# Products of zeros in TensorE's waits through the whole prologue, from a held attention PSUM bank, and the last output tile copied and stored by two engines

## The chip, the cores and the metric

The kernel runs on one core of a Trainium2 chip. The metric is the device time of one launch in microseconds (us). A profiled execution also gives a span, from its first instruction to its last; the time of a launch is about 1.7 us longer than that.

## The reference

A linear-attention recurrence (RWKV-6 style) over 4 batches, 8 heads, 768 steps and head dimension 48, followed by a two-layer MLP on the 3072 rows of 384 that it gives:

```python
def _attn_ref(r, k, v, w, u):
    state = zeros((B, H, D, D)); y = zeros_like(r)
    for t in range(S):
        cur = einsum('bhd,bhe->bhde', u[None] * kt, vt)
        y[:, :, t] = einsum('bhd,bhde->bhe', rt, state + cur)
        state = wt[:, :, :, None] * state + einsum('bhd,bhe->bhde', kt, vt)
    return y

def _moe_ref(x, w_in, w_out):        # x: (3072, 384)
    h = x @ w_in                     # (3072, 2048)
    g = np.maximum(0.01 * h, h)
    return (g @ w_out)               # (3072, 384), float32
```

All inputs are float32; the kernel's matrix products take bfloat16.

## The kernel before, in words

**Attention.** The sequence is cut into 24 chunks of 128 steps (6 a batch). For chunk i the steps are: `log` of the decays w (ScalarE), `cum` (TensorE: running sums of the logs by a triangular matrix, into a PSUM bank), `exp` and `neg`/`exn` (e to the sum and to its negative), `kr` (VectorE: k and r scaled by them, bf16), `trans` (TensorE: eight transposes into the tile `trp`) and `rkT` (their copy to SBUF), `scores` (TensorE, two banks `at`), `m0` and `m1` (VectorE: causal mask), `mix` (TensorE: scores times v, plus the carried state, into `y`), `ysb` (VectorE: y plus the diagonal part), `kv`, `tt` and `st` (the state update: TensorE, VectorE or ScalarE, GpSimd), and `ytr` and `xT` (transposed y as the MLP's input, resident in SBUF). GpSimd computes `t1`, `t2` and `vsc`, VectorE `diag`, for the diagonal part. The first four chunks (EARLY) take another form of `log` and `cum`, from two loads `wp` of two chunks each, and get `neg` from TensorE through a bank of the MLP pool.

**MLP.** The rows are taken in 15 blocks q of 128 or 256. `hid` (q, j) is a group of hidden products for some of the 16 hidden tiles from j on, into a PSUM tile `hp`; `act` is the leaky ReLU out of it (ScalarE); `out` multiplies the result by w_out into a tile `op`. `m_copy` (L479) copies an output tile of 128 x 384 from PSUM to SBUF on ScalarE and `m_store` (L483) issues its store from ScalarE's DMA queue. The weights are loaded in four quarters each and cast to bf16 by VectorE (`cast`).

**PSUM.** Eight banks: the pool `ps_att` has five (tag "att"), `ps_mlp` three (tag "mlp").

**The order.** All instructions are listed with engine, planned duration, needs and the PSUM banks that they take until some later step ends. The class `Order` simulates this list: it repeatedly takes the step that can start first, and keeps for each pool a list of slots with the step that will free each. The kernel is then emitted in exactly that order, and every engine runs its instructions in it. Loads go out on SyncE's DMA queue (SP), as do the transposing DMAs that replace `trans` from chunk 10 and `ytr` from chunk 18 on.

**Zero products.** At emission, before each TensorE step whose predecessor on TensorE ends before WARM (18.0 us of the plan), the planned gap is filled with products of a tile of zeros, `idle`, into the PSUM tile `scratch`: one for each planned 0.45 us before 6.0 us, and for each 0.22 us after it, every one of 512 columns. `scratch` has one of the three MLP banks, a fact that the planner isn't told of.

Of the kernel before, what the change touches and what calls it, by code (L numbers as in the profile page):

```python
# [8 lines left out]
F32 = mybir.dt.float32  # L9
# [6 lines left out]
class Order:  # L16
# [7 lines left out]
    def add(self, name, eng, took, f, *args, lag=0.06, rank=0.0, needs=(), takes=()):  # L24
        self.steps[name] = (eng, took, f, args, lag, rank, list(needs), takes)
# [11 lines left out]
    def run(self, pools):  # L37
        ends, out = {}, []
        self.times = []
        free = {}  # L40
        slots = {p: [None] * n for p, n in pools.items()}
        place = {}
        todo = {}
        for seq, (name, s) in enumerate(self.steps.items()):
            todo.setdefault(s[0], []).append((s[5], seq, name))
        for eng in todo:
            if eng != "DMA":
                todo[eng].sort()
            free[eng] = 0.0
        free["DMA"] = 0.85  # L50

        def ready(name):
            t = 0.0
            for n in self.steps[name][6]:
                n = self.real(n)
                if n not in ends:
                    return None
                same = self.steps[n][0] == self.steps[name][0] != "DMA"
                t = max(t, ends[n] - (self.steps[n][4] if same else 0.0))
            for pool in slots:  # L60
                n = sum(p == pool for p, _ in self.steps[name][7])
                if n:
                    freed = [x for x in slots[pool] if x is None or x in ends]
                    if len(freed) < n:
                        return None
                    freed.sort(key=lambda x: -1 if x is None else place[x])
                    t = max([t] + [ends[x] for x in freed[:n] if x is not None])
            return t

        while any(todo.values()):  # L70
            best = None
            for eng, names in todo.items():
                loads = False
                for rank, seq, name in names:
                    waits = name[0] in ("store", "rkT", "xT")
                    if eng == "DMA" and not waits:
                        if loads:
                            continue
                        loads = True
                    t = ready(name)  # L80
                    if t is None:
                        continue
                    if eng == "DMA" and waits and loads:
                        t += self.slack[name[0]]
                    t = max(t, free[eng])
                    key = (t, rank, seq)
                    if best is None or key < best[0]:
                        best = (key, eng, (rank, seq, name))
            assert best is not None, {e: n[:3] for e, n in todo.items()}
            (t, _, _), eng, item = best  # L90
            todo[eng].remove(item)
            _, took, f, args, lag, _, _, takes = self.steps[item[2]]
            free[eng] = t + took
            ends[item[2]] = t + took + lag
            place[item[2]] = len(place)
            for pool, until in takes:
                freed = [x for x in slots[pool] if x is None or x in ends]
                oldest = min(freed, key=lambda x: -1 if x is None else place[x])
                slots[pool].remove(oldest)
                slots[pool].append(self.real((until, item[2][1]) if isinstance(until, str) else until))  # L100
            out.append((f, args))
            self.times.append((t, t + took, eng))
        self.ends, self.free = ends, free
        return out
# [3 lines left out]
def kernel(  # L108
# [11 lines left out]
    nc = tc.nc  # L120
    B, H, S, D = r.shape
# [9 lines left out]
    NOUT = moe_w_out.shape[1]  # L131
# [3 lines left out]
    NQ = 4  # L135
# [7 lines left out]
    opool = ctx.enter_context(tc.tile_pool(name="opool", bufs=NOUTB))  # L143
    ps_att = ctx.enter_context(tc.tile_pool(name="ps_att", bufs=5, space=bass.MemoryType.PSUM))
    ps_mlp = ctx.enter_context(tc.tile_pool(name="ps_mlp", bufs=3, space=bass.MemoryType.PSUM))
# [6 lines left out]
    idle = const.tile([128, 512], BF16, name="idle")  # L152
# [92 lines left out]
    att = {i: {} for i in range(NCH)}  # L245
# [202 lines left out]
    starts = [sum(sizes[:n]) for n in range(len(sizes))]  # L448
    gts = {}
    hps = {}  # L450
    ops = {}
    osbs = {}
# [23 lines left out]
                start=(j == 0), stop=(j == NFT - 1),  # L476
            )

    def m_copy(q, ts):  # L479
        osb = osbs[q, ts] = opool.tile([128, NOUT], F32, name="osb")  # L480
        nc.scalar.copy(out=osb[:], in_=ops.pop((q, ts))[:])  # L481

    def m_store(q, ts):  # L483
        row = starts[q] + ts * 128
        nc.scalar.dma_start(out=out[row : row + 128, :], in_=osbs.pop((q, ts))[:])

    def m_stored(q, ts):
        pass
# [2 lines left out]

    BY_DMA = range(10, NCH)
    Y_BY_DMA = range(18, NCH)
    WARM = 18.0
    OFF = {'exn': -1.5, 'log': -1.5, 'trans': -2.5, 'ytr': -0.5, 'exp': -2.5, 'scores': -0.5, 't2': 1.5, 't1': -2.5, 'ysb': 1.5, 'vb': 1.5, 'vsc': 1.5}
    RCAST = 5
    SLACK = 1.2
# [3 lines left out]
    add = order.add  # L501
# [6 lines left out]
    for kind, n in queue:  # L508
        past_user = users[-NIN:][:1] if len(users) >= NIN else []
        if kind == "in":  # L510
            if n < EARLY:
                order.alias(("w", n), ("wp", n // 2))
                if n % 2 == 0:
                    add(("wp", n // 2), "DMA", 1.35, load_wp, n // 2, lag=1.95,
                        needs=[("logp", n // 2 - 1)] if n else [])
# [65 lines left out]
    for q, mb in enumerate(sizes):  # L581
        nj = 512 // mb
        xs = [("xT", i) for i in range(starts[q] // L, (starts[q] + mb) // L)]
        for j in range(0, NFT, nj):
            add(("hid", q, j), "PE", nj * 3 * (mb / 2400 + 0.0035), m_hid, q, j, nj, lag=0.17, rank=100 + q,
                takes=(("mlp", ("act", q, j)),),
                needs=xs + [("cast", "w_in", (j + nj - 1) // JQ)] + ([("out", q - 2, sizes[q - 2] // L - 1, NQ - 1)] if q > 1 else []))
            add(("act", q, j), "ACT", nj * mb / 1200 + 0.17, m_act, q, j, nj, rank=RACT, needs=[("hid", q, j)])
        acts = [("act", q, j) for j in range(0, NFT, nj)]
        for ts in range(mb // L):  # L590
            for part in range(NQ):
                add(("out", q, ts, part), "PE", JQ * 0.163, m_out, q, ts, part, lag=0.17, rank=101.5 + q + 0.01 * ts,
                    takes=(("mlp", ("copy", q, ts)),) if part == 0 else (),
                    needs=[x for x in acts if x[2] < (part + 1) * JQ] + [("cast", "w_out", part)]
                    + ([("out", q, ts, part - 1)] if part else []))
            tiles.append((q, ts))
            add(("copy", q, ts), "ACT", 0.48, m_copy, q, ts, rank=0, needs=[("out", q, ts, NQ - 1)]
                + [("store", *x) for x in tiles[-NOUTB - 1 : -NOUTB]])
            add(("issue", q, ts), "ACT", 0.3, m_store, q, ts, rank=-1, needs=[("copy", q, ts)])
            add(("store", q, ts), "DMA", 0.6, m_stored, q, ts, lag=1.9, rank=-1, needs=[("issue", q, ts)])  # L600
    steps = order.run({"att": 5, "mlp": 3})
    with tc.manual_schedule():
        nc.scalar.preload_act_table_set("natural_log_exp_and_others")
        scratch = ps_mlp.tile([128, 512], F32, name="scratch", tag="mlp")
        at = 1.3
        for (f, args), (start, end, eng) in zip(steps, order.times):
            if eng == "PE" and at < WARM:
                for _ in range(int((start - at) / (0.45 if at < 6.0 else 0.22))):
                    nc.tensor.matmul(scratch[:], lhsT=idle[:, 0:128], rhs=idle[:], start=True, stop=True)  # L609
            if eng == "PE":  # L610
                at = end
            f(*args)
# [30 lines left out]
```

## Time and profile before

| | |
|---|---|
| median of 4 runs | 187.65 us |
| lowest, highest | 186.71, 189.6 us |
| the profiled execution: time | 186.71 us |
| the profiled execution: span | 185.0 us |
| TensorE busy | 176.7 us (96%) |
| zero products | 22 records, 8.2 us busy |
| hidden products (line 462) | 720, 72.1 us busy |
| output products (line 474) | 384, 69.5 us busy |

How to read it: PE is TensorE, PEld its weight loads, DVE is VectorE, ACT is ScalarE, POOL is GpSimd, SP is SyncE. In a list of instructions in order of time the first number is the start within the span and the second the length of the merged group, both in us; `x8` counts instructions; brackets give the idle time of the engine just before, and what ended it. [...] In the lists of waits the numbers are total us, times, and the longest.

### The profile page before, as it was taken

Reading aid. Unit: us, or ns where it says so; the run is one execution under the profiler, and the core shown is the slowest. Engines: PE = TensorE matmul, PEld = TensorE weight load, DVE = VectorE, ACT = ScalarE, POOL = GpSimd, SP = SyncE. Lnnn points to the kernel's source line nnn. Section 1 sums busy time; section 2 is a strip of 40 time slices with the busy share of each in tenths; the row PEclk is TensorE's granted clock in tenths of the full one; section 3 lists DMA queues with packets and bytes.
Section 4 is the critical chain, followed back from the end, with each engine's and each line's share of the span. In section 5 each row is a group of like instructions: output and inputs, shape, how many; then the busy total and the mean of one; then the engine's idle time right before and its main releaser. Section 6 shows DMA issues by size and latency. Waiting matters only on the chain.

```text
span 185.0 us, 4892 instructions
## 1 busy us (share of the span) xinstructions
PE 176.7 (96%) x1954; PEld 134.4 (73%) x1955; DVE 113.6 (61%) x187; ACT 113.2 (61%) x218; POOL 109.9 (59%) x144
## 2 busy tenths in 40 slices
PE   7999769999999999999999999999999999999992
PEld 1456558966879878688796688869785786887961
DVE  4368996494689987848495775657575573460000
ACT  3656858914857857677695478669573465662731
POOL 7568975406666799995748785865559268220000
PEclk9999999999999999999999999999999999999999
DMA  6999999999989999998979989899996999422102
GB/s 137 187 211 276 227 348 168 393 351 152 292 173 212 206 199 208 187 224 177 210 149 175 190 178 209 165 200 199 199 160 143 185 180 214 108 64 65 45 7 78
DMA packets 120696, 34.46 MB, mean 186 GB/s; under 512 B 115553, under 2 KB 118626, under 8 KB 120674
## 3 DMA queue, kind: packets, MB, share of 16 engines
q1 hardware_dynamic: 117216, 29.43, 81.8%
q10 hardware_dynamic: 3458, 4.72, 7.6%
q8 instruction: 15, 0.25, 0.6%
q14 instruction: 7, 0.06, 0.1%
HBM read 25.17 MB, written 4.72 MB: 162 GB/s over the span
## 4 chain that ended last, share of the span: by engine, by line
PE 81%; DMA 5%; POOL 4%; DVE 4%; issue 2%; ACT 2%; ACTq 0%; POOLq 0%; DVEq 0%
PE op L474 33%; PE hp L462 31%; PE at L367 3%; DMA rkT<-kr 3%; PE y L392 2%; DMA wp<-in_w_dram 2%; PE trp L346 2%; PE cum L282 2%; PE scratch L609 2%; POOL t L322 2%; PE y L386 2%; PE ytr L433 2%; PE kv L405 1%; DVE mt L375 1%; POOL t L318 1%
## 5 line engine op out<-in xcount | busy, mean ns | idle before, releaser
L462 PE MATMUL hp<-xT,w_in_b 128*128 128x256 bf16 (+1 forms) x720 | 72.1, 252 | 0.5 <-ACT xT L441 0.2
L468 ACT ACTIVATE gt<-hp 128x512 bf16<-128x512 f32 x96 | 56.9, 597 | 21.5 <-PE hp L462 18.2
L474 PE MATMUL op<-w_out_b,gt 128*128 128x384 bf16 x384 | 69.5, 326 | 0.0
L462 PEld LDWEIGHTS <-w_in_b 128*128 128x128 bf16 x720 | 62.8, 114 | 3.9 <-DVE w_in_b L239 0.9
L474 PEld LDWEIGHTS <-gt 128*128 128x128 bf16 x384 | 35.7, 98 | 20.0
L375 DVE TENSOR_TENSOR mt<-at,tri 128x512 bf16<-128x512 f32 x48 | 30.8, 683 | 10.4 <-PE at L367 10.2
L318 POOL TENSOR_TENSOR t<-in,ukb 128x384 f32<-128x384 f32 x24 | 24.0, 1002 | 17.6 <-DMA in<-in_r_dram 8.9
L314 DVE TENSOR_TENSOR kr<-e,in 128x768 bf16<-128x768 f32 x24 | 27.4, 1143 | 10.8 <-ACT e L310 9.6
L423 POOL TENSOR_TENSOR st<-tt,e 48x192 bf16<-48x192 f32 x40 | 22.6, 565 | 14.6 <-DVE tt L413 10.2
L337 POOL TENSOR_TENSOR vsc<-in,diag 128x384 f32<-128x384 f32 x24 | 23.4, 976 | 11.4 <-DVE diag L333 11.0
L322 POOL TENSOR_TENSOR t<-t,in 128x384 f32<-128x384 f32 x24 | 26.0, 1082 | 3.0 <-DMA in<-in_k_dram 1.7
L400 DVE TENSOR_TENSOR ysb<-y,vsc 128x384 bf16<-128x384 f32 x24 | 13.3, 552 | 11.6 <-PE y L392 7.8
L307 ACT ACTIVATE e<-cum 128x388 f32<-128x388 f32 x24 | 11.9, 494 | 13.6 <-PE cum L284 7.6
L481 ACT COPY osb<-op 128x384 f32<-128x384 f32 x24 | 11.4, 477 | 14.2 <-PE op L474 14.0
L329 POOL CAST vb<-in 128x384 bf16<-128x384 f32 x20 | 12.7, 635 | 7.1 <-DMA in<-in_v_dram 6.6
L300 DVE SCALAR_TENSOR_TENSOR neg<-cum,lw 128x384 f32<-128x384 f32 x20 | 11.0, 552 | 9.3 <-ACT e L307 9.1
L333 DVE TENSOR_REDUCE diag<-t 128x8 f32<-128x384 f32 x24 | 13.1, 544 | 5.0 <-POOL t L322 5.0
L254 ACT ACTIVATE lw<-in 128x384 bf16<-128x384 f32 x20 | 10.4, 520 | 5.6 <-DMA in<-in_w_dram 5.4
L310 ACT ACTIVATE e<-neg 128x384 f32<-128x384 f32 x20 | 10.5, 523 | 4.8 <-DVE neg L300 3.1
L441 ACT COPY xT<-ytr 128x384 bf16<-128x384 bf16 x18 | 8.6, 477 | 2.1 <-ACT osb L481 1.2
L367 PE MATMUL at<-rkT 48*128 48x128 bf16 x192 | 9.5, 219 | 0.2 <-DMA rkT<-kr 0.2
L609 PE MATMUL scratch<-idle 128*128 128x512 bf16 x22 | 8.2, 505 | 1.3 <-DVE idle L180 1.3
(55 smaller groups left out, 137.6 us busy)
## 6 DMA issues: line engine op xcount, KB each, us to landing
in<-in_r_dram SPq DMA_DIRECT2D x24, 192.0 KB, 4.4
in<-in_k_dram SPq DMA_DIRECT2D x24, 192.0 KB, 4.6
in<-in_v_dram SPq DMA_DIRECT2D x24, 192.0 KB, 4.7
out_dram<-osb ACTq DMA_DIRECT2D x24, 192.0 KB, 3.1
in<-in_w_dram SPq DMA_DIRECT2D x20, 192.0 KB, 4.7
ws<-in_moe_w_in_dram SPq DMA_DIRECT2D x4, 768.0 KB, 6.5
ws<-in_moe_w_out_dram SPq DMA_DIRECT2D x4, 768.0 KB, 6.5
wp<-in_w_dram SPq DMA_DIRECT2D x2, 384.0 KB, 4.4
```

The lines of the kernel that those rows point to most:

```text
L314: nc.vector.tensor_tensor(out=kr_b[i % NB3][:, :, 0:D], in0=e, in1=ins[i]["kr"], op=ALU.mult)
L318: nc.gpsimd.tensor_tensor(out=t1[:], in0=flat(ins[i]["r"]), in1=ukb[:], op=ALU.mult)
L322: nc.gpsimd.tensor_tensor(out=flat(t2[:]), in0=att[i]["t1"][:], in1=flat(ins[i]["k"]), op=ALU.mult)
L333: nc.vector.tensor_reduce(out=diag[:], in_=att[i]["t2"][:], axis=AX.X, op=ALU.add)
L337: nc.gpsimd.tensor_tensor(out=vsc[:], in0=ins[i]["v"], in1=att[i]["diag"][:].unsqueeze(2).to_broadcast([128, H, D]), op=ALU.mult,)
L367: nc.tensor.matmul(ats[x][:, p, :], lhsT=rkT[r0 : r0 + D, 0, p, :], rhs=rkT[r0 : r0 + D, 1, p, :], start=True, stop=True,)
L375: nc.vector.tensor_tensor(out=att[i]["mt"][:, x], in0=att[i]["ats"][x][:], in1=tri[:].unsqueeze(1).to_broadcast([128, NP, 128]), op=ALU.mult,)
L400: nc.vector.tensor_tensor(out=ysb[:], in0=att[i]["y"][:], in1=flat(att[i]["vsc"][:]), op=ALU.add)
L423: nc.gpsimd.tensor_tensor(out=sn[r0 : r0 + D, :, x * D : (x + 1) * D], in0=tt[r0 : r0 + D, :, x * D : (x + 1) * D], in1=el[r0 : r0 + D, :] ...
L462: nc.tensor.matmul(hp[:, jj, :], lhsT=w_in_b[:, wq, t, f0::JQ], rhs=xT[:, t, t0 : t0 + mb], start=(t == 0), stop=(t == KT - 1),)
L468: nc.scalar.activation(out=gts[q][:, j : j + nj, :], in_=hps.pop((q, j))[:], func=AF.Prelu, alpha=0.01)
L474: nc.tensor.matmul(ops[q, ts][:], lhsT=gts[q][:, j, ts * 128 : (ts + 1) * 128], rhs=w_out_b[:, j, :], start=(j == 0), stop=(j == NFT - 1),)
```

## The change

The zero products go on until 33.0 us of the plan. Each has 256 columns instead of 512, one for each planned 0.22 us where the gap begins before COLD (8.2 us), and for each 0.11 us after it. `scratch` moves to an attention bank, and the planner now knows: one of its five attention slots is held by a step `warm` that ends at 33 us. The two steps `cold` and `warm` on an engine of their own, `CLOCK`, do nothing but mark that time in the order.

The last output tile is split at column 192. ScalarE copies and stores the first half as before; a new VectorE step `copy2` copies the second half into a tile of its own, and `store2` issues its store from SyncE's queue.

```diff
@@ Order.run
         slots = {p: [None] * n for p, n in pools.items()}
+        slots["att"][0] = "warm"
@@ the output tile
-    def m_copy(q, ts):
+    HALF = NOUT // 2
+
+    def m_copy(q, ts, last):
         osb = osbs[q, ts] = opool.tile([128, NOUT], F32, name="osb")
-        nc.scalar.copy(out=osb[:], in_=ops.pop((q, ts))[:])
-
-    def m_store(q, ts):
+        n = HALF if last else NOUT
+        nc.scalar.copy(out=osb[:, 0:n], in_=ops[q, ts][:, 0:n])
+
+    def m_store(q, ts, last):
         row = starts[q] + ts * 128
-        nc.scalar.dma_start(out=out[row : row + 128, :], in_=osbs.pop((q, ts))[:])
+        n = HALF if last else NOUT
+        nc.scalar.dma_start(out=out[row : row + 128, 0:n], in_=osbs[q, ts][:, 0:n])
+
+
+    def m_copy2(q, ts):
+        osb = osbs["last"] = opool.tile([128, HALF], F32, name="osb2", bufs=1)
+        nc.vector.tensor_copy(out=osb[:], in_=ops[q, ts][:, HALF:])
+
+    def m_store2(q, ts):
+        row = starts[q] + ts * 128
+        nc.sync.dma_start(out=out[row : row + 128, HALF:], in_=osbs["last"][:])
@@ constants of the plan
-    WARM = 18.0
+    WARM = 33.0
+    COLD = 8.2
@@ the steps of an output tile
-            add(("copy", q, ts), "ACT", 0.48, m_copy, q, ts, rank=0, needs=[("out", q, ts, NQ - 1)]
+            last = starts[q] + (ts + 1) * 128 == B * S
+            if last:
+                add(("copy2", q, ts), "DVE", 0.28, m_copy2, q, ts, rank=200, needs=[("out", q, ts, NQ - 1)])
+                add(("store2", q, ts), "DMA", 0.4, m_store2, q, ts, lag=1.9, rank=200, needs=[("copy2", q, ts)])
+            add(("copy", q, ts), "ACT", 0.28 if last else 0.48, m_copy, q, ts, last, rank=0, needs=[("out", q, ts, NQ - 1)]
                 + [("store", *x) for x in tiles[-NOUTB - 1 : -NOUTB]])
-            add(("issue", q, ts), "ACT", 0.3, m_store, q, ts, rank=-1, needs=[("copy", q, ts)])
+            add(("issue", q, ts), "ACT", 0.3, m_store, q, ts, last, rank=-1, needs=[("copy", q, ts)])
@@ the end of the list, and the emission
+    warm = []
+    add("cold", "CLOCK", WARM, warm.append, 0)
+    add("warm", "CLOCK", 0.01, warm.append, 1, needs=["cold"])
     steps = order.run({"att": 5, "mlp": 3})
...
-        scratch = ps_mlp.tile([128, 512], F32, name="scratch", tag="mlp")
+        scratch = ps_att.tile([128, 512], F32, name="scratch", tag="att")
         at = 1.3
         for (f, args), (start, end, eng) in zip(steps, order.times):
-            if eng == "PE" and at < WARM:
-                for _ in range(int((start - at) / (0.45 if at < 6.0 else 0.22))):
-                    nc.tensor.matmul(scratch[:], lhsT=idle[:, 0:128], rhs=idle[:], start=True, stop=True)
+            if eng == "PE" and len(warm) < 2:
+                for _ in range(int((start - at) / (0.22 if at < COLD else 0.11))):
+                    nc.tensor.matmul(scratch[:, 0:256], lhsT=idle[:, 0:128], rhs=idle[:, 0:256], start=True, stop=True)
```

## The prediction

> **What bounds the kernel now.** I read the page's busy row first, then busy time by stretch, then TensorE's instructions in order of time with the chain beside them, and last the end.
>
> ```profile
> PE 176.7 (96%) x1954; PEld 134.4 (73%) x1955; DVE 113.6 (61%) x187; ACT 113.2 (61%) x218; POOL 109.9 (59%) x144
> ...
> 18.50:23.10 4.60, 3.58 (x49) 2.70 (x47) 4.34 (x7) 3.88 (x7) 4.37 (x6) 1.00 0.90 227
> 23.10:27.70 4.60, 3.05 (x45) 2.59 (x46) 4.18 (x8) 2.31 (x4) 3.32 (x4) 1.00 1.04 349
> 27.70:32.40 4.70, 4.41 (x50) 4.06 (x45) 2.83 (x5) 3.79 (x9) 2.61 (x3) 1.00 1.11 168
> 32.40:60.00 27.60, 27.60 (x340) 21.82 (x338) 20.04 (x31) 17.08 (x34) 13.85 (x19) 1.00 1.02 263
> 60.00:120.00 60.00, 59.95 (x750) 48.09 (x745) 43.99 (x71) 41.54 (x84) 47.08 (x60) 1.00 0.99 190
> 120.00:181.50 61.50, 61.20 (x607) 47.00 (x604) 27.60 (x44) 34.63 (x67) 25.74 (x34) 1.00 0.70 136
> ```
>
> The first pair after the stretch's length is TensorE. From 32.4 to 181.5 us it idles 0.35 us in all, so whatever moves its entry into this dense part moves the end by as much. Before it TensorE waits: 1.02 + 1.55 + 0.29 = 2.9 us between 18.5 and 32.4. That is all that filling can reach after 18 us.
>
> ```profile
> 7.79 1.46 PE L609 MATMUL scratch<-idle 128*128 128x512 bf16 x3
> 9.04 1.06 PE L346 MATMUL trp<-ident,kr 128*128 128x128 bf16 x8
> 9.90 2.13 PE L609 MATMUL scratch<-idle 128*128 128x512 bf16 x6
> 11.96 0.40 PE L367 MATMUL at<-rkT 48*128 48x128 bf16 x8
> 12.29 0.62 PE L346 MATMUL trp<-ident,kr 128*128 128x128 bf16 x8
> 12.97 0.81 PE L609 MATMUL scratch<-idle 128*128 128x512 bf16 x3
> ...
> 23.17 0.62 PE L346 MATMUL trp<-ident,kr 128*128 128x128 bf16 x8 [0.41 <-DVE kr L314]
> 25.07 0.34 PE L433 MATMUL ytr<-ident,ysb 128*128 128x128 bf16 x3 [1.29 <-DVE ysb L400]
> 25.94 1.50 PE L462 MATMUL hp<-xT,w_in_b 128*128 128x256 bf16 x12 [0.20 <-DVE w_in_b L239]
> 29.95 0.32 PE L282 MATMUL cum<-lw,tri 128*128 128x384 bf16 x1 [0.28 <-ACT lw L254]
> ```
>
> Three products of 512 take 1.46 us at 7.79 and 0.81 at 12.97, eight transposes 1.06 and then 0.62: TensorE is at half speed first, and at full speed from about 11.3 us (inside the group of six). It is never slow again: the transposes at 23.17 still take 0.62. The granted-clock column shows 1.00 throughout and can't tell this; durations do. The chain holds scratch (7.86, 1.40 us; 10.11, 1.93 us), so products on the critical path already cost something. After 14 us the chain runs through GpSimd (vsc, t, st), which is full from 14.2 to 26.6.
>
> ```profile
> DVE neg L300 <- ACT e L307: 9.1, 9, 2.7
> ...
> 181.48 0.48 ACT L481 COPY osb<-op 128x384 f32<-128x384 f32 x1 [2.12 <-PE op L474]
> 181.99 0.34 ACTq L485 DMA_DIRECT2D out_dram<-osb  x1
> ```
>
> `neg` reads `cum` and `lw`, not `e`, yet waits for the exp that reads the same `cum` bank: two readers of one bank on two engines are put one behind the other. The last lines are the tail: copy, issue, 1.9 us to landing by the store's row, then the closing 1.1 us to 185.0.
>
> [...] The rise agrees with the durations above; the worst 3.4 us after it (21.7 to 25.1) is about half busy and the clock held. So there is no clock to win after 18 us here, and the rise may fall elsewhere in another execution. [...] the 60 hidden products at 30.21 take 6.72 us, less a last one's 0.27, over 59 steps: 109 ns. [...]
>
> **The change part by part.** The fills per gap come from the planner: its list stepped through with the code's own costs. These are plans, not measurements; the trace's 3, 2, 3, 6, 3, 5 fills before 18 us confirm the plan's gaps (one record of the fourth group of products is missing: 23 weight loads against 22 products).
>
> *Fills before 18 us.* The gap ahead of the first transposes (planned from 7.57) now falls under COLD: three products of 256 instead of three of 512. A slow transpose of 128 columns takes (1.06 - 0.31) / 7 = 0.107 us, so 256 take 0.213: 0.64 us instead of 1.28; TensorE is free at 8.43, and `kr` ends at 8.55, so the transposes start at 8.6 instead of 9.04: 0.44 us won. rkT (1.01 us on ScalarE) ends at 10.7. But the next gap gets 12 x 256, as many columns as six times 512. From 9.46 they run slow until 11.3 (8.6 of them), then 3.4 x 0.108: free at 11.7. The scores come at 11.75 instead of 11.96: **0.2 us won**, on the chain through mask and diag into GpSimd.
>
> *The held bank.* Of five attention banks four are left until 33 us of the plan. The plan uses the fifth once: cum of chunk 2, while y-transpose, two scores and kv stand. It then waits for `tt`, which ends at 15.08 against a start of 15.02: 0.1 us at most, partly behind exp and kr. In the plan it is 0.4 us later, which shrinks the fill before mix 1 from 10 to 6 and moves four from before scores 2 to before ytr 1. No later step needs a fifth bank before 33, so I take the later order as unchanged. The MLP pool gets a third real bank until 17 us, where `neg` needs one: nothing.
>
> *Fills after 18 us.* About 33 products, 33 x 0.109 = 3.6 us, against 2.9 us of waits, gap by gap (fills against the idle before): ytr 1 and scores 2 together 0.65 against 0.44; mix 2 0.1 to 0.2 against nothing; trans 3 0.44 against 0.41; ytr 2 1.20 against 1.29; hid 4 0.33 against 0.20; hid 8 0.33 against nothing; cum 4 0.55 against 0.28. Most excess is caught: scores 2 waits behind the w_in cast on VectorE (19.70 to 20.65), kv 2 behind `kr`, and the 1.29 ends the lateness at ytr 2. What is queued behind the last fills is late: hid 4, mix 3, hid 8, cum 4, and then hid 12, where the dense part begins. There 0.33 + 0.33 + 0.55 stand against 0.20 + 0.28, less what chain slack takes: I take **0.3 us lost**, between 0 (every wait as long as planned) and 0.75. With the early 0.2 the dense part begins 0.1 us later.
>
> *The tail.* No row shows a half copy. ScalarE: 597 ns for 512 columns, 477 for 384, so 0.94 ns a column and about 0.30 us for 192. VectorE: 683 and 552, so 1.02 ns a column and 0.36 us. Both halves read one bank, and the planner emits ScalarE's first, so VectorE's follows: 181.48 + 0.30 + 0.03 + 0.36 = 182.17, against 181.96 now. SP has only its closing wait left and issues in 0.34. Half the bytes save about 0.1 us of packets (eight per DMA engine at 65 ns, 0.52 us, now). So **0.1 us lost**. If the reads ran side by side the store would start at 181.87, 0.1 earlier, plus packets: 0.25 us won. Bounds -0.25 and +0.25.
>
> Sum: -0.2 + 0.3 + 0.1 = +0.2 us on this execution's 186.71 (span 185.0 and 1.7 around it). The median of the four runs is 0.94 above it; the cause is not visible in one profile, and I carry it over: 187.65 + 0.2, about 187.9 us. A measurement of this kernel tells about 1%, 1.9 us, from no change.
>
> **The rivals.** *The fills become work* (slower). In hardware TensorE comes to these steps 1 to 2 us behind the plan; if the waits of 18 to 30 us shrink, 3.6 us of products stand in an in-order queue ahead of the real steps. Decides when less than half of the 2.9 us remains: 3.6 - 1.3 = 2.3 us lost, 2.2 after the other terms: 189.8. At no waits it would be 3.5: 191.2. For it: hid 4 and hid 8, where fill exceeds idle already. Against: the 1.29 us and 0.41 us waits end on VectorE and GpSimd, which fills don't feed.
>
> [...] The new pause between 8.43 and 8.6 thins the first dense stretch. Scores, transposes and the nine products before mix 0 then run at half speed: mix 0 at 15.1 instead of 13.7. +1.4 + 0.2: 189.3. For it: the earlier stretch from 4.3 to 7.8, nearly all busy but half of it with 64 rows, raised nothing. [...]
>
> *All of it pays* (faster). Every fill fits its wait, the 0.44 us passes whole because the clock rises sooner, and the halves run side by side: -0.44 - 0.25, with at most 0.3 from a steadier clock: 186.7.
>
> **How the numbers follow.** Forecast 0.60 (187.2 to 188.6, by the bounds of fills and tail); fills as work 0.18; clock later 0.10; all pays 0.12. Range: 186.5, the gain and some scatter, to 189.6, which holds the clock case and part of the fills'. Slower by over 1% (above 189.53): 0.15 of fills as work and 0.05 of clock later, 0.20; faster (below 185.77): 0.06 of all pays; the rest, 0.74, within.
>
> **What would show it.** Transposes 0 at 8.6 and scores 0 near 11.75; durations halving near 11.3; cum 2 waiting for `tt`; no idle of over 0.2 us on TensorE from 18 to 33; the first of the long hidden groups at 30.3 (30.21 now); VectorE's half copy starting as ScalarE's ends, and 1.9 us from there to landing. Wrong if that group starts after 31.5 or before 29.5, or if the dense part's order differs.

## The result, and the profile after

The changed kernel is slower: ratio to the kernel before 1.0052, 95% interval 1.0037 to 1.0067, about +1.0 us (medians 188.24 us of 43 runs, 187.12 of 64 in the same comparison). Forecast were +0.2 us, within 1%, 186.5 to 189.6: the time lies inside, and the size was five times too small. The profiled execution took 188.2 us, span 186.5. The comparison leaves out executions more than 1.5% above the fastest of their own kernel; among 188 further executions of the kernel before these were 53, each with a mean granted TensorE clock of 0.987 to 0.991, where it had fallen for a while; in no execution of the changed kernel was it under 0.9955.

Busy time and stretches, first the page's row, then the columns as before (TensorE is the first pair after the length):

```profile
PE 180.9 (97%) x2012; PEld 140.2 (75%) x2012; DVE 114.1 (61%) x188; ACT 112.8 (60%) x218; POOL 108.9 (58%) x144
...
18.50:23.10 4.60, 4.11 (x50) 3.18 (x49) 4.60 (x8) 2.80 (x6) 3.09 (x5) 1.00 0.91 223
23.10:27.70 4.60, 4.51 (x61) 3.59 (x60) 4.22 (x7) 2.57 (x4) 4.45 (x5) 1.00 1.04 356
27.70:32.40 4.70, 4.70 (x60) 4.53 (x59) 3.46 (x5) 3.20 (x7) 2.29 (x4) 1.00 0.82 151
32.40:60.00 27.60, 27.60 (x324) 21.86 (x323) 19.03 (x29) 17.57 (x35) 13.71 (x18) 1.00 1.00 260
```

The waits of 18 to 32 us are filled: 0.58 us of idle are left of 2.9. But the real work is not earlier for it. TensorE in order of time, the changed kernel:

```profile
7.86 0.82 PE L632 MATMUL scratch<-idle 128*128 128x256 bf16 x3
8.68 1.03 PE L347 MATMUL trp<-ident,kr 128*128 128x128 bf16 x8
9.50 2.77 PE L632 MATMUL scratch<-idle 128*128 128x256 bf16 x12
12.20 0.61 PE L368 MATMUL at<-rkT 48*128 48x128 bf16 x8
12.93 0.65 PE L347 MATMUL trp<-ident,kr 128*128 128x128 bf16 x8
...
19.44 0.62 PE L347 MATMUL trp<-ident,kr 128*128 128x128 bf16 x8 [0.49 <-DVE kr L315]
...
20.98 0.33 PE L434 MATMUL ytr<-ident,ysb 128*128 128x128 bf16 x3
...
31.41 0.33 PE L283 MATMUL cum<-lw,tri 128*128 128x384 bf16 x1
31.57 0.24 PE L285 MATMUL cum<-ones,lw 128*128 128x1 bf16 x4
31.67 6.72 PE L463 MATMUL hp<-xT,w_in_b 128*128 128x256 bf16 x60
```

and two lines of the kernel before:

```profile
19.84 0.34 PE L433 MATMUL ytr<-ident,ysb 128*128 128x128 bf16 x3 [0.44 <-DVE ysb L400]
...
30.21 6.72 PE L462 MATMUL hp<-xT,w_in_b 128*128 128x256 bf16 x60
```

The first transposes come at 8.68 instead of 9.04, as intended; the twelve products behind them then all run at about half speed (2.77 us, where twelve of 256 columns take 1.50 at 25.94 in the kernel before), because the clock rises only at 13.0 us in this execution, against 11.3 in the one before. The long hidden group, with which the dense part begins, starts at 31.67 instead of 30.21: +1.46 us, as much as the difference in span (1.5). Of this, 1.14 us are there already at y-transpose 1 (20.98 against 19.84). The tail:

```profile
182.87 0.32 ACT L485 COPY osb<-op 128x192 f32<-128x192 f32 x1 [2.12 <-PE op L475]
183.22 0.34 ACTq L490 DMA_DIRECT2D out_dram<-osb  x1
183.22 0.36 DVE L495 COPY osb<-op 128x192 f32<-128x192 f32 x1 [15.38 <-ACT osb L485]
183.61 0.36 SPq L499 DMA_DIRECT2D out_dram<-osb  x1
```

VectorE's half starts at 183.22, when ScalarE's has ended (182.87 + 0.32 = 183.19), and waits for it by name: these two reads of one bank are in series.

### The profile page after: what moved, and what is told of

Read it like the earlier page. It is cut to its first block, busy times and chain, and to the rows that moved or that the text cites. A ratio compares the mean times of both kernels' runs of the same rounds, so it can differ in the third digit from the quotient of the medians.

```text
span 186.5 us, 5011 instructions
## 1 busy us (share of the span) xinstructions
PE 180.9 (97%) x2012; PEld 140.2 (75%) x2012; DVE 114.1 (61%) x188; ACT 112.8 (60%) x218; POOL 108.9 (58%) x144
## 4 chain that ended last, share of the span: by engine, by line
PE 87%; POOL 4%; DVE 3%; issue 3%; ACT 1%; ACTq 0%; POOLq 0%; DVEq 0%
PE op L475 34%; PE hp L463 32%; PE scratch L632 4%; PE at L368 4%; PE y L393 2%; PE trp L347 2%; PE ytr L434 2%; PE cum L283 2%; PE y L387 2%; PE kv L406 1%; POOL t L323 1%; DVE mt L376 1%; POOL st L424 1%; POOL vsc L338 1%; PE ub L209 1%
## 5 line engine op out<-in xcount | busy, mean ns | idle before, releaser
L319 POOL TENSOR_TENSOR t<-in,ukb 128x384 f32<-128x384 f32 x24 | 25.5, 1064 | 17.8 <-DMA in<-in_r_dram 17.3
L315 DVE TENSOR_TENSOR kr<-e,in 128x768 bf16<-128x768 f32 x24 | 27.5, 1145 | 11.1 <-ACT e L311 9.9
L338 POOL TENSOR_TENSOR vsc<-in,diag 128x384 f32<-128x384 f32 x24 | 21.3, 888 | 12.5 <-DVE diag L334 12.2
L323 POOL TENSOR_TENSOR t<-t,in 128x384 f32<-128x384 f32 x24 | 25.5, 1061 | 2.4 <-DMA in<-in_k_dram 1.3
L401 DVE TENSOR_TENSOR ysb<-y,vsc 128x384 bf16<-128x384 f32 x24 | 13.3, 553 | 12.6 <-PE y L393 8.9
L485 ACT COPY osb<-op 128x384 f32<-128x384 f32 (+1 forms) x24 | 11.3, 470 | 14.4 <-PE op L475 14.1
L632 PE MATMUL scratch<-idle 128*128 128x256 bf16 x80 | 14.5, 322 | 1.3 <-DVE idle L181 1.3
L311 ACT ACTIVATE e<-neg 128x384 f32<-128x384 f32 x20 | 10.5, 523 | 5.1 <-DVE neg L301 3.3
L255 ACT ACTIVATE lw<-in 128x384 bf16<-128x384 f32 x20 | 10.4, 519 | 5.0 <-DMA in<-in_w_dram 4.9
L632 PEld LDWEIGHTS <-idle 128*128 128x128 bf16 x80 | 8.0, 112 | 5.6 <-issue 2.5
```

Source lines behind the costliest of these rows:

```text
L315: nc.vector.tensor_tensor(out=kr_b[i % NB3][:, :, 0:D], in0=e, in1=ins[i]["kr"], op=ALU.mult)
L319: nc.gpsimd.tensor_tensor(out=t1[:], in0=flat(ins[i]["r"]), in1=ukb[:], op=ALU.mult)
L323: nc.gpsimd.tensor_tensor(out=flat(t2[:]), in0=att[i]["t1"][:], in1=flat(ins[i]["k"]), op=ALU.mult)
L338: nc.gpsimd.tensor_tensor(out=vsc[:], in0=ins[i]["v"], in1=att[i]["diag"][:].unsqueeze(2).to_broadcast([128, H, D]), op=ALU.mult,)
L401: nc.vector.tensor_tensor(out=ysb[:], in0=att[i]["y"][:], in1=flat(att[i]["vsc"][:]), op=ALU.add)
L632: nc.tensor.matmul(scratch[:, 0:256], lhsT=idle[:, 0:128], rhs=idle[:, 0:256], start=True, stop=True)
```

## The experiments

All changes are to the kernel before unless said otherwise. Besides the ratio I use the mean granted clock that is listed for each execution. It is 0.996 to 1.000 in most, and 0.980 to 0.991 in the others. e10's profile shows such a fall: a granted clock of 0.51 from 27.0 to 30.4 us, which is 0.49 x 3.4 / 187 = 0.9% of the kernel, and a mean of 0.991. (In the profiles of before and changed, both with a mean of 1.000, the clock falls 0.4 and 0.6 us after the end of the span. A fall 1.5 us ahead of the end would make 0.996, by my estimate: 0.5 x 1.5 / 185.) "Held" means 0.9955 or more. The mean of the held executions is 187.10 us for the kernel before (119 of 188 in three comparisons, 187.05 to 187.14 in each). "w4" is the load of w for chunk 4, "entry" the start of the long hidden group; both, and the second instruction fetch, are from the one profiled execution.

| kernel | ratio, 95% | clock fell | held mean minus 187.10 (± two standard errors) | fetch 2, us | w4 lands, us | entry, us |
|---|---|---|---|---|---|---|
| before | 1 | 69 of 188 | 0 | 29.4 | 29.3 | 30.21 |
| changed | 1.0052 (1.0037 to 1.0067) | 0 of 44 | +1.14 ± 0.21 | 27.3 | 30.3 | 31.67 |
| e1, tail alone | 1.0009 (0.9976 to 1.0042) | 11 of 22 | +0.25 ± 0.47 | 29.5 | 29.6 | 30.42 |
| e2, no tail | 1.003 (1.0001 to 1.006) | 0 of 22 | +1.21 ± 0.40 | 25.8 | 30.0 | 30.88 |
| e3, bank held | 0.9995 (0.9964 to 1.0025) | 4 of 22 | -0.15 ± 0.20 | 29.4 | 29.4 | 30.29 |
| e4, changed, stop at 18 | 1.0036 (1.0002 to 1.0071) | 12 of 22 | +0.85 ± 0.49 | 28.5 | 29.3 | 30.28 |
| e5, early products new | 1.006 (1.0017 to 1.0102) | 7 of 14 | +1.32 ± 0.75 | 27.9 | 30.3 | 31.18 |
| e6, late products alone | 1.0006 (0.998 to 1.0032) | 0 of 22 | +0.48 ± 0.25 | 28.4 | 29.5 | 30.59 |
| e7, half the late ones | 1.0046 (1.0012 to 1.0081) | 2 of 14 | +1.24 ± 0.28 | 28.2 | 30.7 | 31.60 |
| e8, e6 with fewer early | 1.0013 (0.9975 to 1.0051) | 0 of 14 | +0.90 ± 0.49 | 28.5 | 29.3 | 30.46 |
| e9, padded | 1.0074 (1.0042 to 1.0106) | 11 of 20 | +0.62 ± 0.28 | 28.1 | 30.0 | 30.88 |
| e10, early short | 1.0045 (1.0011 to 1.0079) | 10 of 19 | +0.07 ± 0.33 | 28.7 | 30.0 | 32.31 |
| e11, changed, 512 wide | 1.0006 (0.9977 to 1.0035) | 0 of 14 | +0.14 ± 0.38 | 28.1 | 28.9 | 30.33 |
| e12, two gaps | 1.0019 (0.9997 to 1.0042) | 0 of 22 | +0.45 ± 0.24 | 29.0 | 29.5 | 30.33 |

**First question: which part?** e1 takes the tail alone, e2 the change without it, e3 the held bank alone, e4 the change without its late products.

```diff
# e3, to the kernel before (the CLOCK steps are added too)
+        slots["att"][0] = "warm"
-        scratch = ps_mlp.tile([128, 512], F32, name="scratch", tag="mlp")
+        scratch = ps_att.tile([128, 512], F32, name="scratch", tag="att")
# e4, to the changed kernel
-            if eng == "PE" and len(warm) < 2:
+            if eng == "PE" and at < 18.0:
```

> The kernel before with the split of the last output tile alone. My theory (the loss is all in the prologue): ratio to before 1.000 within 0.002; VectorE's half copy starts as ScalarE's ends, and both kernels need 2.44 us from the last output product to the landing. Rival (the tail costs what was worked out, 0.1 us, or more through the extra wait in the closing): ratio 1.0005 to 1.002, not to be told from the first by the ratio, but by a landing 2.5 us or more after the last product.

> The changed kernel with the last tile copied and stored whole, as before. My theory: it keeps the whole loss, ratio to before 1.004 to 1.007, and the long hidden group starts between 30.8 and 31.8 us instead of 30.2. Rival (tail counts): ratio 1.003 or less.

> The kernel before, its own 512-column products up to 18 us of the plan, but scratch in an attention bank that the planner holds until 33 us; no product after 18. Theory A (the held bank makes the loss: the planner delays cum of chunk 2 by 0.4 us, puts the exn of chunk 3 ahead of the copy of xT 1 on ScalarE, and hid 0 comes late): ratio 1.003 to 1.006. Theory B (the late products make it, the bank costs 0.1 us at most): ratio 1.000 to 1.001.

> The changed kernel without the products after 18 us of the plan (about 29 of 82), the bank still held until 33. Theory A (bank): most of the loss stays, ratio 1.003 to 1.006. Theory B (late products): the loss is gone, ratio 0.999 to 1.001, and TensorE idles some 3 us between 18 and 32 us.

The tail is worth nothing that can be seen (e1), and without it the held mean keeps its loss (e2, +1.21). The held bank costs nothing that can be seen (e3). So theory A fell. But B fell too: without late products most of the loss stays, +0.85 ± 0.49 in e4. Besides the split tail, what was left was the one thing that e4 shares with the change and e3 doesn't: the early products in their new form. In e2's profile the clock had risen early, scores 0 came at 11.40 (before: 11.96), and TensorE was through with its last filling at 29.98; yet it then waited:

```profile
29.27 0.71 PE L615 MATMUL scratch<-idle 128*128 128x256 bf16 x5
30.61 0.32 PE L283 MATMUL cum<-lw,tri 128*128 128x384 bf16 x1 [0.64 <-ACT lw L255]
```

**Second question: early or late products?**

```diff
# e5, to the kernel before
-                for _ in range(int((start - at) / (0.45 if at < 6.0 else 0.22))):
-                    nc.tensor.matmul(scratch[:], lhsT=idle[:, 0:128], rhs=idle[:], start=True, stop=True)
+                for _ in range(int((start - at) / (0.22 if at < 8.2 else 0.11))):
+                    nc.tensor.matmul(scratch[:, 0:256], lhsT=idle[:, 0:128], rhs=idle[:, 0:256], start=True, stop=True)
# e6, to e3: its own early rule stays, and after it
+            if eng == "PE" and WARM <= at and len(warm) < 2:
+                for _ in range(int((start - at) / 0.11)):
+                    nc.tensor.matmul(scratch[:, 0:256], lhsT=idle[:, 0:128], rhs=idle[:, 0:256], start=True, stop=True)
# e7, to the changed kernel
-(0.22 if at < COLD else 0.11)
+(0.22 if at < COLD or at >= 18.0 else 0.11)
# e8, to e6
-(0.45 if at < 6.0 else 0.22)
+(0.45 if at < 10.6 else 0.22)
```

> The kernel before, with only its products up to 18 us of the plan made as the change makes them (256 columns, half the columns where the gap begins between 6.0 and 8.2 us, then one for each 0.11 us), scratch still in an MLP bank, nothing after 18 us, the tail whole. Theory P (late products cost the 0.3 us that I worked out, the early ones gain 0.2): ratio 0.998 to 1.0005. Theory Q (the shorter filling ahead of the first transposes makes the clock rise later, and that is most of the loss): ratio 1.002 to 1.006. In both the mean granted clock falls to 0.988 in about a third of the executions, as before.

> The kernel before with its own rule for the products up to 18 us, the held attention bank, and the changed kernel's products of 256 columns from 18 to 33 us; the tail whole. Theory P: the late products alone make the loss where the clock holds, ratio 1.002 to 1.005. Theory Q: they cost 0.3 us, ratio 1.000 to 1.002. In both no execution has a mean granted clock under 0.99, which about a third have without late products.

> The changed kernel with half as many products after 18 us of the plan (14 instead of 34). Theory P: half the loss or less is left, ratio 1.000 to 1.003. Theory Q: the loss stays, ratio 1.003 to 1.006. The granted clock: if half the filling is enough to hold it, no execution is under 0.99; if not, up to a third.

> The kernel of the late products alone, and before 10.6 us of the plan one product of 512 columns for each 0.45 us: one instead of three ahead of the first transposes, three instead of six ahead of the first scores. If TensorE's clock rises as before, the first scores start near 10.8 instead of 12.0 and it gains 0.5 to 1 us on the kernel of the late products alone (ratio to it 0.995 to 0.997); if the rise needs the dense stretch from 7.8 to 11.3, it [...] costs 1 us or more (ratio to it 1.004 to 1.008).

The early products alone carry a loss as large as the change's (e5, +1.32 ± 0.75); the late ones with the held bank make +0.48 ± 0.25 (e6). So far theory Q; but its reason, the clock's rise, is not what e5's profile shows. There the clock rose at 10.4 us, earlier than in the kernel before, y-transpose 3 started at 28.91 (before: 29.34), and then:

```profile
28.91 0.33 PE L433 MATMUL ytr<-ident,ysb 128*128 128x128 bf16 x3
30.92 0.32 PE L282 MATMUL cum<-lw,tri 128*128 128x384 bf16 x1 [1.68 <-ACT lw L254]
```

The log waited for w4, which landed at 30.3. Entry is w4's landing plus 0.86 us, within 0.01, in eight of the fourteen profiles (before, e1, e2, e3, e5, e7, e9, e12). That is a floor under the path. Among the first ten profiles w4 lands at 29.3 to 29.6 in the five with few instructions early (before, e1, e3, e6, e8), and at 30.0 or later in four of the five that have the new early form; e4, the fifth, has it at 29.3.

In the changed kernel's own profile this floor does not set entry. It is 30.33 + 0.86 = 31.19, but the log starts 0.40 us after the landing, behind the activation of a hidden group that came late, and entry is at 31.67:

```profile
30.24 0.60 ACT L469 ACTIVATE gt<-hp 128x512 bf16<-128x512 f32 x1 [0.93 <-PE hp L463]
30.73 0.52 ACT L255 ACTIVATE lw<-in 128x384 bf16<-128x384 f32 x1
```

What differs in the DMA traffic is this. The page of the kernel before lists `q8 instruction: 15` packets, 0.25 MB, 16 KB each. From one to the next the trace has about 250 more instructions of TensorE (they begin at 249, 489 and 719 of its records here; the mean step is 246 to 252 in each of the fourteen profiles, single steps 176 to 311). I call them TensorE's instruction fetches, an inference from the queue's name and from that count. The second stands at 29.4 us in the kernel before, when w4 has landed. The DMA view of 29.3 to 29.6 us of the kernel before (packets, MB, share of 16 engines):

```profile
q1 hardware_dynamic: 286, 0.05, 139.5%
q8 instruction: 1, 0.02, 28.6%
```

and of 27.2 to 27.5 us of the changed kernel:

```profile
q1 hardware_dynamic: 232, 0.09, 105.3%
q8 instruction: 1, 0.02, 20.8%
```

28.6% of 16 engines over 0.3 us is 1.37 us, 20.8% is 1.0 us: the length of the one packet. In the changed kernel it stands while the last quarter of w_in and w4 are on their way. Their issue is as early as before; the landing is not. The row of w4's load in the kernel before and in the changed one:

```profile
L201 SPq DMA_DIRECT2D in<-in_w_dram x1: 718/718/718, 20.5 to 20.5; - x1
...
DMA to landing us min/median/max: 8.8/8.8/8.8
```

```profile
L202 SPq DMA_DIRECT2D in<-in_w_dram x1: 695/695/695, 20.6 to 20.6; - x1
...
DMA to landing us min/median/max: 9.8/9.8/9.8
```

What is late can be read from the trace's completion records. It has sixteen for each load of w, k and v read here, and the landing is the last of them. Fifteenth and sixteenth of w4, in us:

| kernel | 15th | 16th |
|---|---|---|
| before | 29.25 | 29.34 |
| changed | 29.28 | 30.33 |
| e2 | 29.34 | 30.02 |
| e5 | 29.61 | 30.32 |
| e7 | 29.46 | 30.74 |

In the last four one completion of the sixteen is 0.7 to 1.3 us behind the rest, which comes about as early as before. In the eight profiles with w4 at 29.6 or earlier the last step is 0.16 at most. In the kernel before a step of 1.0 us stands in the loads of k and v, which land behind its second fetch (31.36 and 32.38; 32.01 and 33.02). So in the profiles of before and changed a fetch of 1.0 to 1.4 us goes with one late completion of the loads next to it; that the one causes the other was not shown, and the trace doesn't name the engine of either.

Each product is two instructions, weight load and matmul: the trace of the changed kernel has 80 and 80 of 256 columns, that of the kernel before 23 loads and 22 matmul records of 512. The change makes 80 products instead of 23: 114 instructions more.

**Third question: the number of instructions by itself.**

```diff
# e9, to the kernel before: in the first wait (at == 1.3) 25 products of one column and one of 512 for three of 512
+                    n = 1
+                    for _ in range(25):
+                        nc.tensor.matmul(scratch[:, 0:1], lhsT=idle[:, 0:128], rhs=idle[:, 0:1], start=True, stop=True)
# e10, to the kernel before
-(0.45 if at < 6.0 else 0.22)
+(0.45 if at < 8.2 else 0.22)
# e11, to the changed kernel
-(0.22 if at < COLD else 0.11)
+(0.45 if at < COLD else 0.22)
-scratch[:, 0:256], lhsT=idle[:, 0:128], rhs=idle[:, 0:256]
+scratch[:], lhsT=idle[:, 0:128], rhs=idle[:]
# e12, to the kernel before
-            if eng == "PE" and at < WARM:
+            if eng == "PE" and (6.0 <= at < WARM or 21.5 <= at < 24.0):
```

> The kernel before with 23 more products, none of which takes time on the path: in TensorE's first wait (1.3 to 2.7 us) 25 products of one column, 27 ns each, and one of 512 columns stand in place of three of 512. So 46 instructions more come ahead of everything. My theory now (the loss comes from TensorE's instruction fetches[...]: the second, at 29.4 us in the kernel before, moves to some 27.5 us, into the load of w_in's last quarter and of w for chunk 4, which then land a microsecond later): w for chunk 4 lands at 30.0 us or later instead of 29.3, the long hidden group starts 0.5 to 1 us later, ratio 1.003 to 1.006. Rival (the columns and the clock make the loss, not the number of instructions): ratio 0.999 to 1.001.

> The kernel before with one product of 512 columns ahead of the first transposes instead of three: the change's shorter filling there, and four instructions fewer instead of 46 more. Theory of the fetches: the second fetch stays near 29.4 us, w for chunk 4 lands near 29.4 and the ratio is 0.997 to 1.000, against 1.006 for the early products as the change makes them. Rival (the shorter filling delays the clock's rise and that is the loss): ratio 1.003 to 1.006 here too.

> The changed kernel with products of 512 columns in place of pairs of 256: the same time to fill, held bank and split tail, about half the added instructions. Theory of the fetches: most of the loss goes, ratio 0.999 to 1.002, w for chunk 4 lands before 29.8 us. Rival (late products and the held bank block the path): ratio 1.003 to 1.006. In both no execution has a mean granted clock under 0.99.

> A version made from what the runs point to: the kernel before without its five products ahead of 6 us, and with seven of 512 columns in the two longest later waits (two ahead of the transposes of chunk 3, five ahead of the transposes of y of chunk 2), scratch in the MLP bank: four instructions more in all by then. Expected if the two waits are where the clock falls: no execution under 0.99 (a third before), and a ratio of 0.998 to 1.001. If the clock falls elsewhere, a fifth to a third of the executions stay under 0.99. If the first five products matter for the clock's rise, ratio 1.003 or more.

e5 had already set the number of instructions against the columns: up to 18 us it has 47 products of 256 columns where the kernel before has 23 of 512, nearly the same columns in 48 more instructions, and it loses 1.3 us. e9 goes further. Its 46 added instructions take no time where they stand, and the path reaches y-transpose 3 at 29.57, 0.23 later than before, with a clock that rose 0.3 later in this execution. Then it waits, as e2 and e5 do:

```profile
28.23 1.50 PE L462 MATMUL hp<-xT,w_in_b 128*128 128x256 bf16 x12
29.57 0.33 PE L433 MATMUL ytr<-ident,ysb 128*128 128x128 bf16 x3
30.61 0.32 PE L282 MATMUL cum<-lw,tri 128*128 128x384 bf16 x1 [0.72 <-ACT lw L254]
30.88 2.35 PE L462 MATMUL hp<-xT,w_in_b 128*128 128x256 bf16 x20
```

```profile
L201 SPq DMA_DIRECT2D in<-in_w_dram x1: 1146/1146/1146, 20.5 to 20.5; - x1
...
ACT lw L254: 0.3, 1
...
DMA to landing us min/median/max: 9.5/9.5/9.5
```

Its ratio also holds executions with a fallen clock, 11 of 20; the held mean says +0.62 ± 0.28. Two things keep e9 from deciding alone. Its w4 is late in five of the sixteen completions, not in one. The single late completion stands earlier, in the first quarter of w_in (18.98 us, the other fifteen by 17.87; 17.50 in the kernel before), where e9's first fetch is at 14.6 instead of 17.6 us, and the next quarter is issued 1.5 us later. So here it was more likely the first fetch that moved into a load. And e9 thins the filling of the first wait, as e12 does: e12 has four instructions more, and loses 0.45 ± 0.24, which no run explains.

e11 is the counterpart. It has 34 products of 512 columns for 80 of 256, so 22 instructions more than the kernel before instead of 114 (a fifth, not the half that was expected), and 17408 columns instead of 20480. The loss is gone, +0.14 ± 0.38 against +1.14. The fewer columns are not the likely reason: e7 has 15360, in 60 products, and loses 1.24. e11's w4 lands at 28.9, though its second fetch stands at 28.1, as e9's does: its loads are some 0.3 us ahead. So the time of the fetch alone doesn't tell. Over the fourteen profiles, w4 lands at 30.0 or later in five of the six with the second fetch at 28.2 or earlier (not e11), and at 29.6 or earlier in seven of the eight with a later one. The eighth is e10: nothing added, fetch at 28.7 and w4 at 30.0, both against its expectation.

e10's ratio can't be read as a loss where the clock holds, since half of its executions have a fallen clock; its held mean is +0.07 ± 0.33: the shorter filling ahead of the first transposes costs nothing that can be seen there. Its one profile was an execution with the fall, and shows where:

```profile
20.00:23.50 3.50, 2.77 (x40) 2.29 (x39) 3.50 (x6) 2.79 (x6) 3.34 (x4) 1.00 0.85 242
23.50:27.00 3.50, 1.66 (x22) 1.21 (x23) 3.08 (x6) 1.77 (x3) 3.35 (x4) 0.99 0.98 362
27.00:30.40 3.40, 3.40 (x30) 2.68 (x28) 1.81 (x4) 1.20 (x2) 0.26 (x1) 0.51 1.09 230
```

From 23.5 to 27.0 us TensorE is 47% busy (1.66 of 3.5 us), the longest pause 1.28 us; in the next 3.4 us the granted clock (the column before the DMA share) is 0.51: a group of 12 hidden products takes 2.54 us instead of 1.50. No execution shows a fall in e6, e8, e11, e2 or the changed kernel, which fill these waits whole, nor in e12 (0 of 22), with seven products of 512 columns in two waits; with half the late products there are 2 of 14 (e7).

e4 and e8, whose w4 is on time, lose 0.9 us all the same. In both profiles the third fetch (40.5, 40.7 us; 41.8 in the kernel before) stands in the load of w for chunk 5, which lands at 43.1 instead of 42.2. Again one completion of sixteen is late, by 1.1 us (41.97 and 43.08; 42.01 and 43.09), against 0.04 to 0.12 in before, e1, e3, e5 and e12, whose third fetch comes after 41.4 (e10 has 0.63 all the same, with its third fetch at 43.6). e4's TensorE waits for it:

```profile
43.68 0.32 PE L283 MATMUL cum<-lw,tri 128*128 128x384 bf16 x1 [0.70 <-ACT lw L255]
```

This wait is less than half of what e4's profile loses after entry (entry +0.07 us, span +1.8).

In two kernels a part of the loss lies outside the span. The time of a launch is 1.7 us longer than the span in all others (1.8 at most), but in 10 of 44 executions of the changed kernel, and in 6 of 22 of e2, it is 2.0 to 3.2 us longer: on the mean 0.2 us of their 1.1 to 1.2. These two have the most TensorE instructions, and their traces alone have a sixteenth fetch, which begins 0.9 and 0.5 us after the span's end. That the launch waits for it was not tested.

Over all executions the mean is 187.91 us for the kernel before, 188.24 for the changed one, 187.55 for e12 and 187.24 for e11, which beats both (by 0.67 ± 0.40 and 1.0 ± 0.4); e12 beats the kernel before by 0.36 ± 0.28.

## Why the prediction was right or wrong

- *First transposes at 8.6, scores 0 at 11.75.* Right for the first: 8.68. Scores 0 depends on the clock's rise, between 10.4 and 13.3 us over the profiles: 11.40 with the new products at a rise of 10.5 (e2), 12.20 at 13.0 (changed). At nearly the same rise, 11.4 (e4) against 11.3 (before), it is 11.88 against 11.96: 0.1 won, not 0.2.
- *Held bank 0.1 us, later order unchanged.* The cost fits (e3, -0.15 ± 0.20). TensorE's order is the same to the end. But the plan moved more than I saw: three products ahead of cum 2 instead of a wait for `tt`, four ahead of hid 0, exn 3 ahead of xT 1 on ScalarE, and t1 3 ahead of vsc 2 on GpSimd.
- *Late products 0.3 us.* It fits the profiles: from y-transpose 1 to entry 10.69 us in the changed kernel, 10.37 in e4, which is the change without them, and 10.37 before. e6's +0.48 ± 0.25 agrees.
- *Tail 0.1 us lost.* The reads are in series, as said; VectorE's half took 0.36 us as worked out, ScalarE's 0.32 (0.30). From the last output product's end to the last landing it is 2.43 us against 2.44. The term was mis-sized: from issue to landing the half store takes 1.66 us instead of 1.89, so 0.24 saved, not 0.1.
- *The sum.* It failed in a term that wasn't there, and that the time lies in the range is owed to the range's width, not to the sum. I priced a product by its columns and put entry down to TensorE's own queue. Entry in the kernel before was set as much by w4, landing at 29.34, 0.04 us before its log began at 29.38: a transfer with no slack, which the views that I read showed as ScalarE waiting behind its activation. And added instructions have a price that no row of TensorE shows: 0.6 to 1.3 us in e9 and e5, and 1.0 ± 0.4 us between e11 and the changed kernel (0.8 of it in the span). That they act through fetches that move into loads fits the completion records; it was not shown. How much of the change's own loss this is stays open: in its profile the queue, after the late clock, was 0.48 us behind w4's floor.
- *Whatever moves entry moves the end by as much.* This holds in the changed kernel (+1.46 and +1.53 us) and not in general: e4 has +0.07 at entry and +1.8 at the end, e8 +0.25 and +1.3. The dense part has a load without slack of its own in e4's profile (w for chunk 5, a wait of 0.70 us).
- *No clock to win after 18 us.* Wrong in 37% of the executions of the kernel before (69 of 188), if the fall lies there as in e10, the one profile that shows it. I took one profile, in which a half-busy stretch (1.70 of 3.40 us, 21.7 to 25.1) held the clock, for all. The fall costs 2.2 us (mean 189.31 where it fell, 187.10 where it held), and the change does away with it (0 of 44). "The cause is not visible in one profile" was true of the 0.94 us between profile and median, and should have widened the faster side.
- *Rivals.* Fills as work named a similar loss by the wrong means: the products do not hold the path beyond 0.3 us. The clock rising late did occur in the changed kernel's profile (13.0 us, 1.7 later than before), and y-transpose 1 is 1.14 us late there. But it is not shown to come from the change: the rise is at 10.4 to 13.0 us in the five profiles with the new early form and at 10.4 to 13.3 in the other nine, and e2 and e5, with an early rise, still have entry 0.67 and 0.97 us late, behind w4. By the prediction's own mark, entry after 31.5, the steps were wrong in the changed kernel's profile.

What stays open: on which engine a fetch and a late completion ran, which the trace doesn't say; why the clock rises and falls when it does; what e12's 0.45 us is; and how the change's 1.1 us divide between the loads, the late products and the closing. Each fetch time and landing is from one execution of its kernel; only the held means rest on many.

## What to carry to other kernels

Count instructions, not only time. e9's 46 more took no time where they stand in TensorE's first wait, and its held mean is 0.62 ± 0.28 us higher, with w4 at 30.0 instead of 29.3; that fetches moved into loads there is an inference. Try filler of few, wide instructions: 34 products of 512 columns cost 0.14 ± 0.38 us here (e11), 80 of 256 cost 1.14 ± 0.21. Look for loads that land just as their reader starts, as w4 does in the kernel before, by 0.04 us. Before saying that a clock has nothing to give, look at the granted clock of many executions, not of one: it held in the one profile of the kernel before, and fell in 69 of 188 executions.

## What the runs showed of the hardware

- The packets of queue q8 are 16 KB each, take 0.88 to 1.51 us in the traces of the kernel before and the changed one, and stand 246 to 252 TensorE instructions apart on the mean of each of the fourteen profiles. The loads of w, k and v read here have sixteen completions; next to such a packet one of them was 0.7 to 1.3 us late (w4 in the changed kernel, e2, e5, e7), but not each time (e11: packet at 28.1, w4 at 28.9); in the eight profiles with w4 at 29.6 or earlier the last step was 0.16 us at most.
- In e10 the granted clock was 0.51 from 27.0 to 30.4 us, after 3.5 us in which TensorE was 47% busy with no pause over 1.28 us. After stretches of 55% in the kernel before (1.88 of 3.40 us, 21.5 to 24.9) and of 49% in e5 (27.5 to 30.9 us, longest pause 1.64) it did not fall.
- The clock rose between 10.4 and 13.3 us in the fourteen profiles: at 11.3 in the kernel before, where TensorE had been 97% busy from 4.4 to 7.8 us (3.31 of 3.40), and at 13.0 in the changed one. What sets the time of the rise, and why the clock fell in only some executions of a kernel, was not shown.
